# Constants behind the second load of x, and filter tables spread over the slots, in a Fourier filter with a soft mixture of experts

## The chip, the cores and the metric

The kernel runs on one core of one Trainium2 chip. The metric is the time of one execution in microseconds (us); three executions of the kernel before were timed. The profile is of one further execution. TensorE is PE in the profile, VectorE DVE, ScalarE ACT, GpSimd POOL, and SyncE, which issues nearly all transfers, SP.

## The reference

```python
def _attn_ref(x, filt_r, filt_i):            # x: (8, 2496, 256)
    X = np.fft.rfft(x, axis=1)
    Y = X * (filt_r + 1j * filt_i)[None, :, :]
    return np.fft.irfft(Y, n=x.shape[1], axis=1)

def _moe_ref(x, phi, w1, w2):                # x: the (19968, 256) rows of the above
    logits = x @ phi                         # 32 slots: 8 experts x 4
    d = softmax(logits, over all rows)       # written out in the original
    slot_input = d.T @ x
    slot_out = relu(slot_input[e] @ w1[e]) @ w2[e]   # for each expert e
    c = softmax(logits, over the slots)
    return c @ slot_out
```

Every sequence is filtered along its length in the frequency domain, and the result goes through a soft mixture of experts whose first softmax runs over all rows of all eight sequences.

## The kernel before, in words

The transform of length 2496 is done as 39 x 64. For each of the eight sequences ("batches" below, numbered from 0) there are three steps. First, eleven units `s1_unit(b, u)` (u = 0 to 10) multiply two blocks of x by a 39-point transform (line 305 for batch 0, in one matmul; line 308 for the others, in three matmuls of a high and a low part that `split_x` makes on ACT, line 294, and on POOL, line 295). Each unit's result is copied out of PSUM into a tile `at`, of which there are five, by ACT (line 312) or DVE (line 310), and written to a scratch array `a_dram` (line 316; the eleventh unit by lines 318 and 319). Second, ten "slots" per batch, `x_unit(b, c)`, each need one tile `ash` that `load_ash` reads back from `a_dram` (line 329) in another order. A read-back of a batch can start only when all of that batch's writes have landed, because every row of `ash` crosses all of them. The slot multiplies `ash` with `b_t` (line 339) and then with the filter tables `fr_t` and `fi_t` on DVE and POOL (lines 352 to 358). Third, `t_unit` (two slots later) transposes the result (line 366) and makes logits (line 377). Once a group of batches is through, a `chain` of small steps computes its softmax and its part of the slot inputs; it is advanced in hops, two per slot. At the end come the experts, and the blocks of the output are written out.

x comes in six loads per batch (`load_x`): each is a transfer of 112 rows and one of 5 rows, 448 and 20 KB (half of that for the sixth). Batch 0 has six buffers for them, the other batches share three (`XB`), so the fourth load waits until a buffer's two units have been split. `next_x` issues the next of these loads; it is called in the list below and after every second split.

Constants: `cst_t` (columns 0 to 128 hold the identity; 64.5 KB; the rest comes at slot 10, line 758), `b_t[:, 0]` (64 KB) and `be_t` (148 KB), from which `build_b` makes the other nineteen matrices of `b_t`, each by one ACT multiply (line 621) and one DVE operation (line 622). `build_minv` transposes the matrices of `b_t` on PE (line 628). `phi_t` and `fny_t` are small. The filter tables come in ten pairs (`load_tables`, lines 639 and 640; 128 KB for `fr_t`, 128 KB for `fi_t`); slot c uses pair c.

Two things set the order of the work. The string `STEPS` lists what is issued after each of the eleven units of batch 0, once before the units of batch 1, and after each of the five "slots" from -5 to -1, which run units 0 to 4 of batch 1. One word belongs to one place; a letter is I (identity), B (`b_t[:, 0]` and `be_t`), P (`phi_t`), F (`fny_t`), C (one `build_b`, two matrices), T (one pair of tables), X (`next_x`), A (one read-back of batch 0), and "-" for nothing. Tables that are left over (`late`) are loaded one pair per slot from slot 0. Besides, the kernel is built with a planner that orders each engine's instructions by their place in the program and by the time at which it thinks they can run; so an instruction can stand earlier on its engine than the program has it. Each engine, and SP's queue of transfers, then runs in the planned order and waits at the first instruction that isn't ready.

Of the kernel before, what the change touches and what calls it, by code (L numbers as in the profile page):

```python
# [9 lines left out]
F32 = mybir.dt.float32  # L10
# [3 lines left out]
AX = mybir.AxisListType  # L14
# [5 lines left out]
NT = 20  # L20
# [22 lines left out]
P = 128  # L43
SCALE = 2.0 / SEQ

XC = 4
# [13 lines left out]
WL = 5  # L60
SB = 3


STEPS = "IB P FC TC TC TC C XC C XC CC AA X - - - ATATAT"


def run_of(i, j):
# [152 lines left out]
def fft_soft_moe(ctx, tc, x, fr, fi, fny, phi, w1, w2, cst, w1q, bmat, out):  # L220
    nc = tc.nc
    pe, dve, act, pool_e, sp = nc.tensor, nc.vector, nc.scalar, nc.gpsimd, nc.sync
# [15 lines left out]
    cst_t = const.tile([P, CST.shape[1]], F32, name="cst_t")  # L238
    b_t = const.tile([P, NT, P], F32, name="b_t")
# [16 lines left out]
    def open_pool(name, bufs, side):  # L256
        cm = tc.tile_pool(name=name, bufs=bufs, side=side, reuse_waits="tile")
        return cm, cm.__enter__()
# [3 lines left out]
    x0_cm, x0p = open_pool("x0p", 6, "left")  # L262
# [9 lines left out]
    def load_x(b, c):  # L272
        pool = x0p if b == 0 else proda
        t = pool.tile([KR, XC, DIM], F32, tag="xt", name=f"xt{b}_{c}", bufs=6 if b == 0 else XB)
        i0 = c * XC
        n = min(XC, NI - i0)
        for lo, hi in ((0, RX), (RX, KR)):
            sp.dma_start(t[lo:hi, 0:n, :], x[b, lo:hi, i0 : i0 + n, :])
        xts[b, c] = t
# [5 lines left out]
    def split_x(b, u):  # L285

        c, k = divmod(2 * u, XC)
        xs = xts[b, c][:, k : k + 2, :]
        if b < FB:
            xhl[b, u] = xs, None  # L290
            return
        xh = proda.tile([KR, 2, DIM], F32R, tag="xh", name=f"xh{b}_{u}", bufs=3)
        xl = proda.tile([KR, 2, DIM], F32R, tag="xl", name=f"xl{b}_{u}", bufs=3)
        act.copy(xh, xs)  # L294
        pool_e.tensor_tensor(out=xl, in0=xs, in1=xh.bitcast(F32), op=ALU.subtract)  # L295
        xhl[b, u] = xh, xl
# [354 lines left out]
    def next_x():  # L651
        if xnext:
            load_x(*xnext.pop(0))

    def split_next(n):
        for b, u in at_slot.get(n, ()):
            split_x(b, u)
            if u % 2 == 1 or u == NH - 1:
                next_x()

    for c in range(6):
        load_x(0, c)
    if WM:
        warm = x0p.tile([P, 512], F32, name="warm", bufs=1)
        dve.memset(warm, 0.0)
        pw = ps_c.tile([P, 512], F32, tag="c", name="warm_up")
        for k in range(WM):
            pe.matmul(pw, warm[:, 0:P], warm, start=True, stop=True)
# [1 line left out]
    b_next = iter(range(CPB))  # L670
    ash_next = iter(range(ASH))
    issue = {
        "I": lambda: sp.dma_start(cst_t[:, 0 : P + 1], cst[:, 0 : P + 1]),
        "P": lambda: sp.dma_start(phi_t, phi.rearrange("(h q) e -> q h e", q=P)),
        "B": lambda: (sp.dma_start(b_t[:, 0], bmat[:, 0:P]), sp.dma_start(be_t, bmat[:, P:])),
        "F": lambda: sp.dma_start(fny_t, fny),
        "C": lambda: build_b(next(b_next)),
        "T": lambda: load_tables(next(tabs_next)),
# [2 lines left out]
    }  # L681
    steps = iter(STEPS.split())

# [2 lines left out]
            if token != "-":  # L686
                issue[token]()

    be_t = x0p.tile([P, 2 * P + 2 * NT], F32, name="be_t", bufs=1)
    split_x(0, 0)  # L690
    for u in range(NH):
        if u + 1 < NH:
# [58 lines left out]
    for n in range(NS + LT):  # L751
# [20 lines left out]
        if n >= LT:  # L772
            b, c = divmod(n - LT, CPB)
# [189 lines left out]
```

## Time and profile before

| | |
|---|---|
| timed executions | 431.23 us median (430.06 to 432.34, three) |
| profiled execution | 425.78 us, of which the span from the first to the last instruction is 423.9 us |
| busy share of the span | PE 88%, DVE 64%, ACT 52%, POOL 48% |
| mean granted TensorE clock | 0.944 of full speed |
| moved by transfers | 107.07 MB, 253 GB/s on average |

In rows of a timeline the first number is the start in us from the span's start, the second the length; "x12" stands for twelve instructions of one kind in a run. The rows of the chain of waits are pieces of the chain of work that ended last, followed back from the end of the kernel. In a table of stretches the share after the clock is the mean busy share of the 16 transfer engines; it can pass 1 a little.

### The profile page before, as it was taken

The page shows a single profiled execution, that of the slowest core. Times are in us where ns is not written, and L with a number is a line of the kernel's source. Part 1 is how long each engine was busy: PE and PEld are TensorE (multiplying, and loading weights), DVE is VectorE, ACT ScalarE, POOL GpSimd, SP SyncE. Part 2 cuts the span into 40 slices and gives each one's busy share as a digit, 9 for nine tenths or more (in the row PEclk, how much of TensorE's full clock was granted, in tenths as well). Part 3 has the DMA queues.
Part 4 walks back from the last instruction along what each step waited for, and adds up shares of the span by engine and source line. Part 5 has one row for each costly group of instructions (what it writes and reads, how often), then busy time and mean ns, then how long its engine had stood idle before and what let it go on. Part 6 is the DMA issues. An engine that isn't in the chain of part 4 may idle for free.

```text
span 423.9 us, 12672 instructions
## 1 busy us (share of the span) xinstructions
PE 374.5 (88%) x5065; PEld 291.3 (69%) x5065; DVE 269.8 (64%) x496; ACT 218.6 (52%) x475; POOL 201.9 (48%) x234
## 2 busy tenths in 40 slices
PE   7557998999999999999989999989998799999740
PEld 2225876788877787886867688778767435898730
DVE  1341764886989955878998387896378322787330
ACT  2465666676677656765792333461446121675320
POOL 0027778797768655965966056572200401750000
PEclk9688999999999999999999999999998999999555
DMA  8999999999889686978996524333199895699994
GB/s 209 238 306 288 331 321 327 334 294 344 246 262 337 213 264 206 289 214 256 269 280 167 186 82 121 101 103 101 55 344 347 268 275 185 249 394 381 386 362 166
DMA packets 61820, 107.07 MB, mean 253 GB/s; under 512 B 6142, under 2 KB 37758, under 8 KB 60226
## 3 DMA queue, kind: packets, MB, share of 16 engines
q1 hardware_dynamic: 61762, 106.26, 79.3%
q8 instruction: 40, 0.66, 0.6%
q14 instruction: 18, 0.15, 0.1%
HBM read 63.50 MB, written 42.74 MB: 251 GB/s over the span
## 4 chain that ended last, share of the span: by engine, by line
PE 61%; DMA 16%; DVE 12%; ACT 3%; issue 2%; SPq 2%; POOL 0%; ACTq 0%; DVEq 0%
PE x L339 15%; PE s L308 8%; PE t L366 6%; DMA out<-obr 6%; DMA xt<-in_x 6%; PE s L581 4%; PE l L377 4%; PE out L903 3%; PE v L423 3%; PE dt L537 2%; DMA ash<-a_dram 2%; DVE t L353 2%; PE o L833 2%; PE lg L450 2%; PE s L305 2%
## 5 line engine op out<-in xcount | busy, mean ns | idle before, releaser
L295 POOL TENSOR_TENSOR xl<-xt,xh 117x512 fp32r<-117x512 f32 x77 | 103.0, 1350 | 52.7 <-ACT xh L294 49.9
L339 PE MATMUL x<-b_t,ash 128*128 128x128 f32 x640 | 91.5, 284 | 6.1 <-DMA ash<-a_dram 3.1
L339 PEld LDWEIGHTS x<-b_t,ash 128*128 128x128 f32 x640 | 81.2, 194 | 17.0 <-issue 5.0
L356 POOL TENSOR_TENSOR yt<-yt,t 128x256 f32<-128x256 f32 x80 | 65.9, 826 | 40.7 <-DVE t L353 30.5
L352 DVE TENSOR_TENSOR yt<-x,fr_t 128x512 f32<-128x512 f32 x80 | 54.7, 684 | 39.9 <-PE x L339 36.9
L294 ACT CAST xh<-xt 117x512 fp32r<-117x512 f32 x77 | 46.8, 622 | 35.4 <-DMA xt<-in_x 12.1
L368 ACT COPY y<-t 128x512 f32<-128x512 f32 x80 | 46.5, 591 | 34.3 <-PE t L366 28.6
L312 ACT COPY at<-s 120x512 f32<-120x512 f32 x83 | 48.4, 587 | 21.7 <-PE s L305 8.6
L353 DVE TENSOR_TENSOR t<-x,fi_t 128x512 f32<-128x512 f32 x80 | 54.3, 678 | 0.0
L366 PE MATMUL t<-cst_t,yt 128*128 128x128 f32 x320 | 48.5, 276 | 0.7 <-POOL yt L356 0.4
L355 DVE TENSOR_TENSOR yt<-yt,t 128x256 f32<-128x256 f32 x60 | 43.3, 730 | 0.8
L366 PEld LDWEIGHTS t<-cst_t,yt 128*128 128x128 f32 x320 | 37.3, 141 | 7.9 <-issue 3.1
L308 PE MATMUL s<-xh,w1h 117*120 117x512 f32 x77 | 36.0, 468 | 6.5 <-ACT xh L294 5.5
L903 PE MATMUL out<-so_h,st 32*128 32x256 f32 (+1 forms) x320 | 36.3, 329 | 3.3 <-ACT obr L912 2.4
L903 PE MATMUL out<-so_l,st 32*128 32x256 f32 (+1 forms) x320 | 34.4, 311 | 0.0
L903 PEld LDWEIGHTS out<-so_h,st 32*128 32x128 f32 (+1 forms) x320 | 29.9, 206 | 6.5 <-ACT obr L912 3.0
L308 PE MATMUL s<-xl,w1h 117*120 117x512 f32 x77 | 32.2, 419 | 0.3 <-POOL xl L295 0.2
L308 PE MATMUL s<-xh,w1l 117*120 117x512 f32 x77 | 31.1, 404 | 0.0
L355 POOL TENSOR_TENSOR yt<-yt,t 128x256 f32<-128x256 f32 x20 | 16.2, 811 | 30.5 <-DVE t L353 24.2
L903 PEld LDWEIGHTS out<-so_l,st 32*128 32x128 f32 (+1 forms) x320 | 30.3, 209 | 0.0
L377 PE MATMUL l<-yt,phi_t 128*32 128x128 f32 x640 | 26.1, 278 | 0.9 <-ACT y L368 0.7
L912 DVE COPY ob<-out 128x512 f32<-128x512 f32 x32 | 20.6, 684 | 7.6 <-PE out L903 7.3
(118 smaller groups left out, 552.6 us busy)
## 6 DMA issues: line engine op xcount, KB each, us to landing
ash<-a_dram SPq DMA_DIRECT2D x80, 256.0 KB
a_dram<-at SPq DMA_DIRECT2D x80, 240.0 KB
xt<-in_x SPq DMA_DIRECT2D x40, 448.0 KB
w<-in_w SPq DMA_DIRECT2D x64, 256.0 KB
out<-ob SPq DMA_DIRECT2D x12, 1024.0 KB
out<-ob SPq DMA_DIRECT2D x8, 512.0 KB
out<-obr SPq DMA_DIRECT2D x8, 448.0 KB
xt<-in_x SPq DMA_DIRECT2D x8, 224.0 KB
```

The source lines that it names most:

```text
L294: act.copy(xh, xs)
L295: pool_e.tensor_tensor(out=xl, in0=xs, in1=xh.bitcast(F32), op=ALU.subtract)
L308: pe.matmul(ps, w, xx, start=(n == 0), stop=(n == 2))
L312: act.copy(at, ps)
L339: pe.matmul(ps[:, 2 * k + dh].rearrange("q r c -> q (r c)"), ash[:, k, dh * P : (dh + 1) * P], b_t[:, t0 + k, :], start=True, stop=True,)
L352: dve.tensor_tensor(out=yt, in0=ps, in1=frv, op=ALU.mult)
L353: dve.tensor_tensor(out=t2, in0=ps[:, :, ::-1, :], in1=fiv, op=ALU.mult)
L355: add.tensor_tensor(out=yt[:, :, 1, :], in0=yt[:, :, 1, :], in1=t2[:, :, 1, :], op=ALU.add)
L356: pool_e.tensor_tensor(out=yt[:, :, 0, :], in0=yt[:, :, 0, :], in1=t2[:, :, 0, :], op=ALU.subtract)
L366: pe.transpose(pt[:, k, dh, :], yt[:, c % 2, 2 * k + dh].rearrange("q r c -> q (r c)"), ident)
L368: act.copy(y, pt.rearrange("k p h d -> k p (h d)"))
L903: nc.tensor.matmul(prs[k][0:rows, mm, :], st[q, n // 2, c0 : c0 + rows], (so_h, so_l)[n % 2][q, :], start=(n == 0), stop=(n == 3),)
```

## The change

The identity, `b_t[:, 0]` and `be_t` are issued within the loop over the six loads of batch 0's x, behind the second load, instead of by the letters I and B after the first unit. The string is rewritten: one pair of tables stands ahead of the first two read-backs (by the string it was three), three more stand among the slots -4 to -1 (three before), and so six pairs instead of four are left for one per slot from slot 0 on. The letters X stand elsewhere, and there are four instead of three.

```diff
-STEPS = "IB P FC TC TC TC C XC C XC CC AA X - - - ATATAT"
+STEPS = "P F C C C C C XC C C CC XTAA AX T A X ATT"
...
+    be_t = x0p.tile([P, 2 * P + 2 * NT], F32, name="be_t", bufs=1)
     for c in range(6):
         load_x(0, c)
+        if c == 1:
+            sp.dma_start(cst_t[:, 0 : P + 1], cst[:, 0 : P + 1])
+            sp.dma_start(b_t[:, 0], bmat[:, 0:P])
+            sp.dma_start(be_t, bmat[:, P:])
...
     issue = {
-        "I": lambda: sp.dma_start(cst_t[:, 0 : P + 1], cst[:, 0 : P + 1]),
         "P": lambda: sp.dma_start(phi_t, phi.rearrange("(h q) e -> q h e", q=P)),
-        "B": lambda: (sp.dma_start(b_t[:, 0], bmat[:, 0:P]), sp.dma_start(be_t, bmat[:, P:])),
...
-    be_t = x0p.tile([P, 2 * P + 2 * NT], F32, name="be_t", bufs=1)
```

## The prediction

> **What bounds the kernel now.** I read the chain of waits first, for the stretch that the change touches (0 to 75 us):
>
> ```profile
> 1.23 0.33 SPq L278
> ...
> 2.32 0.33 SPq L278
> ...
> 2.69 6.71 DMA xt<-in_x
> ...
> 9.42 0.35 SPq L673
> ...
> 9.81 5.10 DMA b_t<-in_bmat
> ```
>
> ```profile
> 34.28 4.37 DMA ash<-a_dram
> ...
> 38.69 3.59 PE x L339 x16
> ...
> 54.53 5.98 DMA xt<-in_x
> ...
> 65.37 5.91 DMA ash<-a_dram
> ...
> 71.32 1.17 PE x L339 x8
> ```
>
> So the path runs through transfers up to 71 us. The first read-back is issued at 34.28, slot 0 begins at 38.69; the read-back for slot 10 (batch 1) is issued at 65.37 and its matmuls begin at 71.32. Then the order of SP's transfers:
>
> ```profile
> 0.74 0.44 SPq L232 DMA_DIRECT2D w1q_t<-in_w1q  x1
> 1.23 6.72 SPq L278 DMA_DIRECT2D xt<-in_x  x12
> 9.42 0.35 SPq L673 DMA_DIRECT2D cst_t<-in_cst  x1
> 9.81 0.43 SPq L675 DMA_DIRECT2D b_t<-in_bmat  x1
> 11.49 0.33 SPq L675 DMA_DIRECT2D be_t<-in_bmat  x1
> ...
> 13.69 0.37 SPq L316 DMA_DIRECT2D a_dram<-at  x1
> ...
> 28.40 0.39 SPq L319 DMA_DIRECT2D a_dram<-at  x1
> 28.84 0.30 SPq L278 DMA_DIRECT2D xt<-in_x  x1
> 29.61 0.36 SPq L639 DMA_DIRECT2D fr_t<-in_fr  x1
> ...
> 33.10 0.75 SPq L278 DMA_DIRECT2D xt<-in_x  x2
> 33.89 0.35 SPq L640 DMA_DIRECT2D fi_t<-in_fi  x1
> 34.28 0.90 SPq L329 DMA_DIRECT2D ash<-a_dram  x2
> ...
> 60.53 0.28 SPq L319 DMA_DIRECT2D a_dram<-at  x1
> ```
>
> The transfer issued at 2.69 is the sixth (`w1q_t`, then four of x at 1.23 to 2.32). It lands at 9.40, and only then, at 9.42, goes the fourteenth: SP holds an issue until the one eight places earlier has landed. `b_t` goes at 9.81 and takes 5.10 us, behind x. All six pairs of tables of `STEPS` stand ahead of the first read-back at 34.28: the planner pulled the three of "ATATAT" forward into SP's wait for the last write of 28.40.
>
> What that does to the engines:
>
> ```profile
> PE minv L628 <- DMA b_t<-in_bmat: 5.4, 1, 5.4
> ```
>
> PE's queue holds the first transpose for `build_minv` (line 628) between units 3 and 4, so PE stands 5.4 us for `b_t` although x is there. It looks like the price of the old order. Whether it is shows in the table of stretches:
>
> ```profile
> 3.00:12.00 9.00, 6.63 (x13) 2.16 (x11) 0.70 (x2) 1.17 (x2) 0.00 (x0) 0.98 1.03 265
> 12.00:18.00 6.00, 2.96 (x5) 1.35 (x6) 1.74 (x5) 2.05 (x6) 0.00 (x0) 0.50 0.88 215
> 18.00:30.00 12.00, 7.17 (x21) 3.35 (x20) 6.45 (x18) 7.64 (x22) 1.25 (x2) 0.93 0.98 302
> 30.00:36.00 6.00, 5.28 (x25) 3.88 (x24) 0.17 (x1) 5.82 (x12) 6.00 (x10) 0.82 0.86 265
> 36.00:60.00 24.00, 21.63 (x177) 18.41 (x176) 15.01 (x26) 12.73 (x25) 16.85 (x17) 0.93 1.02 318
> 60.00:75.00 15.00, 12.75 (x96) 8.80 (x94) 6.26 (x13) 10.71 (x22) 12.34 (x11) 1.00 1.03 334
> 75.00:100.00 25.00, 24.71 (x234) 20.61 (x235) 20.57 (x33) 17.89 (x37) 22.00 (x21) 1.00 1.04 324
> 100.00:160.00 60.00, 58.83 (x852) 48.44 (x854) 50.47 (x80) 39.84 (x83) 41.40 (x39) 1.00 0.87 270
> 160.00:340.00 180.00, 169.25 (x2758) 135.05 (x2756) 130.48 (x248) 89.25 (x200) 87.20 (x99) 0.99 0.65 199
> ```
>
> The first column is the stretch, then each engine's busy time, the clock, the share of the transfer engines, GB/s. From 3 to 100 us the transfers are full except in 12:18 (0.88) and 30:36 (0.86). PE is full from 75 us to 340 us (24.71 of 25, 58.83 of 60, 169.25 of 180), but in 60:75 it has 12.75 of 15. So up to slot 10 the transfers are the bound, and PE afterwards. The last write of batch 1 shows it too: it waits in SP's queue, for a load of x:
>
> ```profile
> SPq L319 <- DMA xt<-in_x: 1.2, 1, 1.2
> ```
>
> **The change part by part.** I count a gain only where it moves the 65.37 us at which slot 10's read-back is issued; PE carries the rest from there at its own pace, so what is won there is won at the end.
>
> Sizes, from the list of transfers:
>
> ```profile
> xt<-in_x SPq DMA_DIRECT2D x40, 448.0 KB
> ...
> fr_t<-in_fr SPq DMA_DIRECT2D x10, 128.0 KB
> ...
> be_t<-in_bmat SPq DMA_DIRECT2D x1, 148.0 KB
> ...
> cst_t<-in_cst SPq DMA_DIRECT2D x1, 64.5 KB
> b_t<-in_bmat SPq DMA_DIRECT2D x1, 64.0 KB
> ```
>
> *Constants moved.* Three issues leave the places 14 to 16 and take 6 to 8. Their issue takes 0.35 + 0.43 + 0.33 = 1.1 us of SP, in which SP would otherwise have waited for landings (9.42 waits on 9.40). They are moved past eight transfers of x. Their 276.5 KB (64.5, 64, 148) cost about 1.1 us at the 265 GB/s of 3:12, by which the third to sixth load of x come later; between 0.6 us (half) and 5.1 us (the whole landing of `b_t`, if small transfers hold up what follows). PE has that slack: it stood until `b_t` was there at 14.91. `b_t` should land near 9 us instead of 14.9, so PE's 5.4 us for it goes; next in line is x itself, two units per load, each load some 1.8 us at 265 GB/s, so PE goes on waiting, in smaller pieces. ACT and DVE can begin `build_b` some 6 us earlier, beside those waits. The first write of `a_dram` moves from 13.69 to about 11, when its turn of eight comes. On the transfers this wins only the hole of 12:18, which comes of three constants and two still smaller transfers (phi, fny) being in flight together: 0.12 x 6 = 0.7 us (bounds 0 and 0.7).
>
> *Fewer tables ahead of the first read-backs.* Up to 34.28 there were six pairs, 12 issues, 1.5 MB. The new string has four before slot 0, one ahead of the read-backs; the planner may again pull the others forward, so two to five pairs fewer, 0.52 to 1.31 MB, 1.7 to 4.3 us at the 302 GB/s of 18:30. With the 0.7 that brings the first read-back to between 29 and 32 us and slot 0 to 33.5 to 36.5 us. That is not yet won: the same bytes must be through before slot 10.
>
> *Tables one per slot.* Six pairs instead of four go in slots 0 to 5: four more issues of 0.36 us ahead of the writes of batch 1 and the loads of batch 2 in SP's queue, 0.52 MB, 1.6 us at 318 GB/s. What waits behind them are writes of `at`, and through them ACT's copies, and the read-back of slot 10. In sum to 65.37 the bytes are unchanged, so I put 0 for it; bounds -0.5 (the idle time of an issue filled) to +1.6. The tables themselves arrive in time: pair 4 + n is issued in slot n, four slots ahead, of (71.32 - 38.69) / 10 = 3.3 us each, against landings of 4.4 to 6 us in the rows above.
>
> *The hole of 30:36.* SP stands for the last write with the queue running dry: 0.14 x 6 = 0.84 us. Two effects: it can vanish as the writes end earlier and spread better, or grow, since tables were what filled SP's wait (28.84 to 33.89). Together with 0.02 x 12 = 0.24 us in 18:30 that is 1.1 us at stake; I take all of it, since the string still has an X and a T directly ahead of the read-backs and the writes of batch 1 to follow. Bounds: gain 1.1, loss 4.2 (below).
>
> *The fourth X.* There are three buffers; a load can't start before its buffer is free, so one more letter only puts it earlier in the order. 0, bounds 0.5 either way (one issue of about 0.3 us and its neighbour).
>
> Sum: 0.7 + 1.1 + 0 + 0 = 1.8 us won of the profiled 425.78 (span 423.9 and 1.9 around it), which would be 424.0. The runs shown have a median of 431.23, 5.4 us above the profiled execution; the same 1.8 taken from it gives **429.4 us**, -0.4%. What tells from no change in a measurement of this kernel is about 0.5%, 2.2 us, so the likeliest case lies close to that bound.
>
> **The rivals.**
>
> *PE's wait was the price* (chance 0.22). If read-backs and writes of batch 1 simply come earlier with PE, the whole 5.4 us arrive: 425.8 us. For it: the chain goes through `b_t`, and writes of `at` that lie in SP's queue go earlier. Against it: full transfers in 36:60 and 60:75.
>
> *Nothing moves* (0.18). The two holes close and others open, such as at slot 10, where the later tables stand ahead of batch 1's writes: 431.2 us. For it: the bytes don't change. Against: the hole of 12:18 has a plain cause that is removed.
>
> *SP stands at the first read-back without filling* (0.15, the slower case). Between the last write (28.40) and the read-back (34.28) the rows show issues of x and of tables: six tables of 128 KB and one load of x, 1.26 MB, 4.2 us at 302 GB/s. If the queue has nothing to send there, these 4.2 us are idle and the bytes come after slot 0, on a bound that is full. With the 0.7 won before: +3.5, 434.7 us; it decides when 2.9 of the 4.2 us are empty (2.2 + 0.7), from which on the case is over 0.5% slower.
>
> *Small transfers hold up the queue* (0.05). The constants take 5.1 us from issue to landing as a train, and the third load of x waits for all of it: then units 4 to 10 begin no earlier than the 14.91 of now, the 0.7 is not won, and 1.1 is left: 430.1. The Trainium skill, "DMA: Bandwidth & Descriptors" (Anatomy of one DMA, and Measured), speaks for that: for transfers that GpSimd issues it gives a fixed part of about 2.0 us each and advises batches of 1 MiB or more. As an estimate by that page, three transfers served singly would take 6.6 us. By that rule 6.6 us would fall on x. The trace agrees only in part: the share of 1.03 in 3:12, with transfers of 10 to 448 KB in flight, shows them overlapping.
>
> **How the numbers follow.** The forecast has 0.40, with 427.5 to 431.0 as its own range (gain of the two holes doubled, or nearly lost). Of it some 0.18 lie beyond 0.5% faster; with the first rival that is 0.40 and I say 0.41. Slower: 0.15 and a few per cent of the others, 0.18. The remaining 0.41 is no change. The range reaches to the first rival (425.8, less 0.3) and toward the slower one: 425.5 to 433.6, which leaves out about half of each of these two, 2 in 10.
>
> **What would show each step.** PE's wait of line 628 for `b_t` is under 1.5 us, and `b_t` lands near 9 us. The share of 12:18 is 0.95 or more. The first read-back is issued between 29 and 32 us. The read-back for slot 10 is issued at 63 to 64.5 us, and PE waits more than 2.3 us in the 15 us ahead of it (15 - 12.75 now). From there to the end the distance is as before. The prediction is wrong if slot 10's read-back moves with PE by 4 us or more (first rival), or if the share in the 6 us ahead of the first read-back falls under 0.5 (slower case), or if PE loses time after 100 us, which no step here touches.

## The result, and the profile after

The changed kernel is not faster, as forecast, but slightly slower: the ratio of its time to that of the kernel before is 1.0064 with an interval of 1.0037 to 1.009, medians 430.5 against 429.61 us over 20 executions of each. In a second series on another occasion it was 1.0017 (0.9977 to 1.0057); the two, weighted by their intervals, give 1.0050 (1.0028 to 1.0072), about 2.1 us. The ratios leave out executions over 1.5% above the fastest of the same kernel, six of the profiles below are of such ones, and two readings hang on it: by the means of all executions the change is at 1.0027 (0.9993 to 1.0061), not clear of noise, and the fourth load with a buffer (below) at 1.0080 and not at 1.0038. The profiled execution took 432.04 us, its span is 429.9 us.

In the rows of the changed kernel all line numbers of the loop bodies are one lower (L338 is the old L339). Its chain of waits, for the first 110 us:

```profile
3.56 4.86 DMA be_t<-in_bmat
...
15.47 4.28 DMA xt<-in_x
...
19.83 0.04 ACT xh L293
...
20.36 0.59 ACT at L311
...
32.14 5.09 DMA ash<-a_dram
...
37.28 1.43 PE x L338 x8
...
62.42 5.55 DMA xt<-in_x
...
71.34 1.35 PE x L338 x8
...
101.04 7.09 DMA xt<-in_x
```

SP's order of transfers at the places that the prediction speaks of:

```profile
2.69 0.35 SPq L664 DMA_DIRECT2D cst_t<-in_cst  x1
3.08 0.43 SPq L665 DMA_DIRECT2D b_t<-in_bmat  x1
...
12.26 0.36 SPq L315 DMA_DIRECT2D a_dram<-at  x1
...
27.26 0.35 SPq L318 DMA_DIRECT2D a_dram<-at  x1
...
32.14 1.52 SPq L328 DMA_DIRECT2D ash<-a_dram  x3
...
65.12 3.14 SPq L328 DMA_DIRECT2D ash<-a_dram  x4
```

What PE waited for in the first 39 us:

```profile
PE s L304 <- ACT at L311: 3.8, 3, 3.1
PE x L338 <- DMA ash<-a_dram: 1.7, 1, 1.7
...
PE minv L627 <- DVE b_t L621: 0.2, 1, 0.2
```

So the first part went nearly as said: `be_t` has landed by 8.42 us, the 5.4 us for `b_t` are gone, the first read-back goes at 32.14 instead of 34.28, and slot 0 begins 1.4 us earlier. In place of `b_t`, PE now waits 3.8 us for ACT's copies. The longest of these waits ends at 20.99: in the chain above, the load of x issued at 15.47 lands, a split on ACT (L293) takes it at 19.83, and only behind that comes the copy of 20.36 that PE waits for. Then hardly anything comes of it at slot 10: its read-back goes at 65.12 (65.37 before) and PE begins it at 71.34 (71.32). From there on this profile loses. The table of stretches, with the same columns as in the prediction:

```profile
3.00:12.00 9.00, 8.40 (x18) 3.42 (x17) 3.19 (x11) 3.56 (x12) 0.00 (x0) 1.00 1.05 272
12.00:18.00 6.00, 5.55 (x12) 1.59 (x10) 4.20 (x13) 3.71 (x11) 0.00 (x0) 1.00 1.01 290
18.00:30.00 12.00, 8.53 (x26) 4.26 (x27) 1.38 (x2) 7.30 (x15) 6.22 (x7) 0.86 1.01 325
30.00:36.00 6.00, 4.59 (x18) 2.41 (x16) 0.00 (x0) 4.43 (x9) 4.55 (x7) 1.00 0.98 306
36.00:60.00 24.00, 21.50 (x177) 18.45 (x178) 15.10 (x25) 14.19 (x28) 17.72 (x17) 0.93 1.02 316
60.00:75.00 15.00, 12.80 (x89) 8.86 (x86) 7.52 (x12) 8.00 (x16) 9.41 (x9) 0.89 0.99 294
75.00:100.00 25.00, 24.18 (x216) 20.21 (x217) 20.63 (x34) 16.29 (x34) 20.10 (x19) 1.00 1.04 321
100.00:160.00 60.00, 56.30 (x826) 46.38 (x824) 47.99 (x78) 38.19 (x81) 40.59 (x37) 1.00 0.87 259
160.00:340.00 180.00, 168.54 (x2761) 134.49 (x2763) 130.24 (x249) 91.05 (x205) 88.44 (x100) 1.00 0.65 197
```

Both holes of the transfers are closed (12:18 from 0.88 to 1.01, 30:36 from 0.86 to 0.98), and PE loses where the prediction had it full: 0.5 us in 75:100 (24.18 against 24.71) and 2.5 us in 100:160 (56.30 against 58.83). PE waits there for ACT and for DVE. First ACT. A piece of ACT's timeline of the changed kernel, in brackets the idle time before and what ended it:

```profile
101.74 0.30 ACT L383 COPY lt<-l 128x128 f32<-128x128 f32 x1
104.34 1.14 ACT L293 CAST xh<-xt 117x512 fp32r<-117x512 f32 x2 [2.30 <-DMA xt<-in_x]
105.39 0.58 ACT L311 COPY at<-s 120x512 f32<-120x512 f32 x1
105.87 0.59 ACT L367 COPY y<-t 128x512 f32<-128x512 f32 x1
108.82 0.62 ACT L293 CAST xh<-xt 117x512 fp32r<-117x512 f32 x1 [2.36 <-DMA a_dram<-at]
109.34 0.54 ACT L429 COPY v<-v 128x462 f32<-128x462 f32 x1
```

and of PE's in the same stretch:

```profile
106.51 0.65 PE L376 MATMUL l<-yt,phi_t 128*32 128x128 f32 x16 [0.65 <-ACT y L367]
...
109.93 0.90 PE L422 MATMUL v<-minv_t,lsb 128*32 128x66 f32 x48 [0.92 <-ACT v L429]
```

ACT's queue holds a split of x (L293) ahead of copies that PE needs now. The split waits 2.3 us for its x, and the copies of `y` and `v` wait behind it, and PE behind these. ACT's waits for x in 75 to 165 us add up (total, number, longest) to 5.2 us before:

```profile
ACT xh L294 <- DMA xt<-in_x: 5.2, 6, 1.7
```

and to 10.9 us after, with 2.4 us more that the profile puts down to another transfer and that I take to be of the same kind:

```profile
ACT xh L293 <- DMA xt<-in_x: 10.9, 8, 2.3
ACT xh L293 <- DMA a_dram<-at: 2.4, 1, 2.4
```

Of PE's waits over 0.2 us in 75 to 165 us, the two for ACT make 1.6 us (0.7 and 0.9). The longest single one is for DVE:

```profile
PE t L365 <- DVE yt L354: 2.1, 1, 2.1
```

It ends at 144.39 us, and the chain of waits shows what stood ahead on DVE: two subtractions of the `chain` (L487, L603), between and behind which come the filter steps of the slots:

```profile
135.10 3.16 DVE d L487 x3
...
139.46 2.15 DVE lg L603 x2
...
142.80 1.45 DVE yt L354
...
144.39 0.63 PE t L365 x4
```

The second profile of the changed kernel has the same wait of 2.1 us; in the two of the kernel before PE's waits for DVE there are 0.2 us.

Why the split stands there is seen in the order that the planner made of each program. Counting PE's instructions, 53 units of batches 1 to 7 stand ahead of slot 40 (the first of batch 4) in the kernel before, 56 in the changed one. That order is fixed in the program: ACT's and DVE's too is the same in both profiles of the kernel before, and another in both of the changed one, far behind the place of the edit. By the description of the planner above, the edit changed it because the planner places each instruction by when it expects its inputs; what it expected is not on record.

The two profiles differ by 6.0 us of span, more than the times do. Of this 3.0 us are there at the first matmul of the experts (342.97 against 339.97), and the rest arises in the output, which moves from one execution to the next (below). Neither repeats: the second pair of profiles has 341.44 against 343.30 at the experts and spans of 424.2 against 430.4 us. PE's loss in 100:160 does repeat (56.69 against 58.01), that in 75:100 does not (24.95 against 24.35). And a part of it is no loss, since PE has done more by then:

```profile
0.00:39.00 39.00, 24.08 (x65) 11.89 (x66) 10.21 (x28) 19.62 (x45) 9.38 (x16) 0.87 0.91 256
```

in the kernel before, and in the changed one

```profile
0.00:39.00 39.00, 30.22 (x82) 14.13 (x83) 10.12 (x29) 21.90 (x49) 12.43 (x19) 0.94 0.96 285
```

### The profile page after: what moved, and what is told of

Read it like the earlier page. It is cut to its first block, busy times and chain, and to the rows that moved or that the text cites. A ratio compares the mean times of both kernels' runs of the same rounds, so it can differ in the third digit from the quotient of the medians.

```text
span 429.9 us, 12668 instructions
## 1 busy us (share of the span) xinstructions
PE 379.8 (88%) x5065; PEld 292.9 (68%) x5065; DVE 269.2 (63%) x496; ACT 218.2 (51%) x475; POOL 201.7 (47%) x234
## 4 chain that ended last, share of the span: by engine, by line
PE 57%; DVE 16%; DMA 16%; ACT 3%; issue 3%; SPq 1%; POOL 0%; ACTq 0%; DVEq 0%
PE x L338 14%; PE s L307 8%; DMA out<-obr 6%; PE t L365 6%; DMA xt<-in_x 5%; PE s L580 4%; PE out L904 4%; PE l L376 3%; DMA ash<-a_dram 3%; DVE t L352 3%; PE v L422 2%; DVE yt L351 2%; DVE yt L354 2%; PE lg L449 2%; DVE d L487 2%
## 5 line engine op out<-in xcount | busy, mean ns | idle before, releaser
L338 PE MATMUL x<-b_t,ash 128*128 128x128 f32 x640 | 91.1, 284 | 6.6 <-DMA ash<-a_dram 1.7
L338 PEld LDWEIGHTS x<-b_t,ash 128*128 128x128 f32 x640 | 81.1, 194 | 16.8 <-issue 4.9
L293 ACT CAST xh<-xt 117x512 fp32r<-117x512 f32 x77 | 46.8, 624 | 36.7 <-DMA xt<-in_x 18.0
L904 PE MATMUL out<-so_h,st 32*128 32x256 f32 (+1 forms) x320 | 38.4, 338 | 6.4 <-ACT obr L913 5.3
L904 PEld LDWEIGHTS out<-so_h,st 32*128 32x128 f32 (+1 forms) x320 | 31.5, 215 | 9.0 <-ACT obr L913 6.0
L904 PE MATMUL out<-so_l,st 32*128 32x256 f32 (+1 forms) x320 | 36.3, 319 | 0.0
L904 PEld LDWEIGHTS out<-so_l,st 32*128 32x128 f32 (+1 forms) x320 | 31.9, 217 | 0.0
```

The lines of the kernel that those rows point to most:

```text
L338: pe.matmul(ps[:, 2 * k + dh].rearrange("q r c -> q (r c)"), ash[:, k, dh * P : (dh + 1) * P], b_t[:, t0 + k, :], start=True, stop=True,)
L904: nc.tensor.matmul(prs[k][0:rows, mm, :], st[q, n // 2, c0 : c0 + rows], (so_h, so_l)[n % 2][q, :], start=(n == 0), stop=(n == 3),)
```

## The experiments

The theories: the *fourth load* (one X more puts loads and units of later batches ahead in the planned order); the *constants* (`build_minv`'s transposes, now ahead of unit 2 in PE's queue, upset what follows); the *tables* (late ones are in the way); *chance* (two single executions differ). All ratios are against the kernel before.

**The changed kernel again, and the kernel before again**

> The changed kernel once more, to see which of its losses repeat. In the two profiles at hand it begins slot 0 1.4 us earlier than the kernel before (37.3 against 38.7), slot 10 at the same time, slot 79 3.3 us later (293.5 against 290.2), and ends 6.0 us later, so 2.7 us more in the output. Fourth-load theory and constants theory: the 3.3 us up to slot 79 repeat to 1 us, since they come of the order of the instructions. Chance theory (the difference lies in states of single executions): slot 79 moves by more than 2 us. All theories: the 2.7 us of the output may be of one execution only. Time against before: ratio 1.004 to 1.009 by the first two, 0.997 to 1.009 by the last.

> The kernel before once more, for how far a single profile moves: slots 10, 40 and 79 within 1.5 us of 71.3, 168.4 and 290.2 us; the output from its first matmul (359.9) to the end (423.9) may differ by 6 us, as it did between the two profiles of the changed kernel.

Measured: the changed kernel 1.0017 (0.9977 to 1.0057), with a span of 424.2 us, slot 10 at 70.0 and slot 79 at 292.0. The ratio lies below what I had put down for an effect of the order (1.004 to 1.009) and in the range for chance (0.997 to 1.009). The kernel before (one further profile) has a span of 430.4, slots 10, 40 and 79 at 72.1, 170.8 and 293.8. So slot 79 of one and the same kernel moves by 3.6 us from execution to execution, more than I had allowed (1.5), and slot 79 of a single profile can't decide between the theories, though I had set bounds by it. From the first output matmul to the end it took 64.1 and 65.2 us in the two profiles of before, 66.8 and 63.0 in those of the changed kernel: the 2.7 us in the output were of one execution. What repeats is ACT's wait for x, 5.2 and 5.7 us in the two profiles before, 10.9 and 9.1 us after, and PE's wait of 2.1 us for DVE. In what follows the ratios decide, and ACT's waits and PE's busy time say where.

**Constants alone** (edit against the changed kernel)

```diff
-STEPS = "P F C C C C C XC C C CC XTAA AX T A X ATT"
+STEPS = "- P FC TC TC TC C XC C XC CC AA X - - - ATATAT"
```

> Constants behind the second load of x, the string of the kernel before (without I and B). Constants theory (the transposes of build_minv now stand ahead of unit 2 and upset what follows): the whole loss, ratio 1.005 to 1.01, slot 79 at 292 to 294 us, PE busy 56 to 57.5 of the 60 us in 100 to 160. Fourth-load theory: no loss, ratio 0.995 to 1.002, slot 79 at 288 to 290.5, PE busy 58.5 or more of 60 there. Both: slot 10 within 1 us of 71.3, and PE's wait of 5.4 us for b_t is gone.

> The constants alone once more, to narrow the interval of 0.9936 to 1.0. The prediction's sum (1.8 us of 430, 0.9958) holds if the ratio lies in 0.993 to 0.999; no gain if it lies at 0.999 or above. Slot 10 at 69 to 70 us (71.3 and 72.1 before), for a read-back that goes some 2 us earlier.

Measured: 0.9968 (0.9936 to 1.0), and in the repetition 0.9952 (0.9904 to 1.0); weighted together 0.9963 (0.9936 to 0.9990), a gain of 1.6 us. The constants theory falls. Units ahead of slot 40: 53, as before. Slot 10 is at 69.2 and 70.9 (71.3 and 72.1 before), the first further from 71.3 than the 1 us that I had allowed. Its read-back is at 63.8 and 64.8 (65.4 and 66.2), 1.5 us earlier on average, which agrees with the time; but two profiles of each can't show it by themselves, since in the three of the next kernel that read-back goes at 65.4, 66.2 and 61.5.

```profile
12.00:18.00 6.00, 5.70 (x13) 1.87 (x12) 4.07 (x13) 4.16 (x12) 0.00 (x0) 1.00 0.90 241
...
30.00:36.00 6.00, 4.47 (x19) 2.46 (x17) 0.00 (x0) 5.87 (x13) 5.33 (x7) 0.99 1.03 323
```

In this profile of the constants alone the hole of 12:18 is hardly smaller (0.90), the hole of 30:36 is gone (1.03). The second profile agrees (0.85 and 1.02). But the second profile of the kernel before has 0.95 in 30:36, so a part of that hole was of one execution. PE was busy for 58.4 of the 60 us in 100 to 160, between the two expectations; slot 79, at 292.0, lay where the constants theory had it, but slot times don't decide here.

**The changed kernel without its fourth X** (edit against the changed kernel)

```diff
-STEPS = "P F C C C C C XC C C CC XTAA AX T A X ATT"
+STEPS = "P F C C C C C XC C C CC XTAA AX T A - ATT"
```

> The changed kernel without the fourth X (the one after slot -2 is taken out), so that loads of x are issued as early as in the kernel before. Fourth-load theory (one load earlier lets the planner put the units of line 307 some three units earlier in PE's queue, and PE stands there for x in 75 to 160 us): the loss goes, ratio 0.994 to 1.002, slot 79 at 288.5 to 291, no wait of PE or ACT for x over 5 us near 101 us, PE busy 58 or more of the 60 us in 100 to 160. Constants theory: loss stays, ratio 1.004 to 1.01, slot 79 at 292.5 to 294.5. Tables theory (late tables are in the way): loss stays too.

> The changed kernel without the fourth X once more, for a second profile, since the first was of a disturbed execution. Fourth-load theory: slot 79 at 289 to 292 us, and ACT's waits for x in 75 to 165 us under 7 us. Else slot 79 again at 294 or later.

> The changed kernel without its fourth X once more, for the interval: constants and tables as in the change, 54 units ahead of slot 40. If tables placed so cost nothing of their own and the constants gain: 0.993 to 0.999, the same as the constants alone to 0.3%. If the tables take the gain back: 0.999 to 1.003.

Measured: 0.9971 (0.9933 to 1.0009) and 0.9947 (0.9891 to 1.0003), together 0.9963 (0.9932 to 0.9995). The loss is gone, and the gain is that of the constants alone. 54 units stand ahead of slot 40. Slot 79 came at 294.8, 290.6 and 291.4. The wait of ACT for x in 75 to 165 us, of the second and the third profile:

```profile
ACT xh L293 <- DMA xt<-in_x: 3.1, 3, 1.4
```

```profile
ACT xh L293 <- DMA xt<-in_x: 3.9, 4, 1.8
```

One letter, issued at slot -2, is worth 0.9% of the whole time (1.0050 against 0.9963). Tables placed as in the change cost nothing when this letter is out.

**The kernel before with a fourth X**

```diff
-STEPS = "IB P FC TC TC TC C XC C XC CC AA X - - - ATATAT"
+STEPS = "IB P FC TC TC TC C XC C XC CC AA X - - X ATATAT"
```

> The kernel before with a fourth X (after slot -2), nothing else. Fourth-load theory: the loss appears without the constants and tables, ratio 1.004 to 1.01, slot 79 at 292 to 294.5 us, a wait for x of more than 5 us in 95 to 130 us. Constants theory and tables theory: ratio 0.998 to 1.003, slot 79 at 289 to 291.

Measured: 1.0146 (1.0091 to 1.0202), 6.2 us, above the range of 1.004 to 1.01 that I had put down, and three times the loss of the changed kernel. 58 units stand ahead of slot 40.

```profile
ACT xh L294 <- DMA xt<-in_x: 13.0, 8, 3.2
```

**The new string alone, constants at their old place**

```diff
-STEPS = "IB P FC TC TC TC C XC C XC CC AA X - - - ATATAT"
+STEPS = "IBP F C C C C C XC C C CC XTAA AX T A X ATT"
```

> The new string of the changed kernel with the constants left at their old place (I and B in front of its first P). Fourth-load theory, with the constants themselves a gain of 0.3%: the loss is here and larger than in the changed kernel, ratio 1.007 to 1.016, ACT's waits for x (line 294) over 9 us in 75 to 165 us, against 5.2 in the kernel before. If the tables that come later are a gain of their own: less than the 1.0146 of the kernel before with a fourth X, by 0.3% or more; if they are a loss: more by as much. If the loss of the changed kernel needed the constants at the new place: ratio 0.997 to 1.003.

Measured: 1.0101 (1.0056 to 1.0145); 59 units ahead; ACT's waits for x 11.0 us. The loss doesn't need the constants at the new place. Whether the tables gain or lose beside the fourth X is not told by 1.0101 against 1.0146, since the intervals overlap.

**Tables alone**

```diff
-STEPS = "IB P FC TC TC TC C XC C XC CC AA X - - - ATATAT"
+STEPS = "IB P FC C C C C XC C XC CC TAA X - - - ATATAT"
```

> The kernel before with only the tables moved: one pair ahead of the first read-backs and three at slot -1, six late (TAA X - - - ATATAT), three X as before, constants at their old place. In the planned order 58 units of line 307/308 stand ahead of slot 40 in PE's queue here, as with the fourth X (58), against 53 in the kernel before. The prediction's term for tables (nothing, the bytes are the same) and the theory that it is the letter X as such: ratio 0.997 to 1.004, ACT's waits for x in 75 to 165 us 4 to 7 us. The theory that any edit costs which puts splits and units ahead of their loads in the planned order: ratio 1.007 to 1.016, ACT's waits for x over 9 us.

Measured: 1.0117 (1.0052 to 1.0182), 5.0 us, with three X and the constants where they were. So it is not the letter X as such. By the string three pairs of tables no longer stand ahead of the first X, and the planner again puts more units ahead, as it would if it thought that x comes earlier: 58 units, and

```profile
ACT xh L294 <- DMA xt<-in_x: 12.2, 8, 3.7
```

**The fourth load with a buffer of its own**

```diff
-XB = 3
+XB = 4
...
-YB = 34
+YB = 32
```

once on the kernel before with a fourth X, once on the changed kernel. `YB` counts the buffers of `y`, which later hold weights of the experts; two of them make room for the fourth buffer of x.

> The kernel before with a fourth X and with four buffers for it (XB = 4; to make room, ypool has 32 buffers and not 34, which concerns weights after 290 us). The theory that the loss comes of ACT's splits standing earlier in its order than x can land, since the earlier load has no buffer to go to: with a buffer of its own the load goes out at once, ACT's waits for x in 75 to 165 us fall back under 7 us and the ratio to 0.993 to 1.004. The theory that transfers are simply full in that stretch, whatever the buffers: the loss stays, ratio 1.009 to 1.018, ACT's waits stay over 10 us. The theory that it is PE's order alone (units of later batches ahead of slots): loss stays or grows, with ACT's waits small.

> The changed kernel with four buffers for its four X (XB = 4, ypool 32 buffers). Theory of ACT's splits waiting for a load without a buffer: the loss goes while the constants' gain stays, ratio 0.992 to 1.001, ACT's waits for x in 75 to 165 us under 6 us (9.1 and 10.9 in the changed kernel). Else ratio 1.002 to 1.01. In the planned order units stand even further ahead here (61 ahead of slot 40), so a theory of PE's order alone expects 1.005 or more.

Measured: 1.0038 (1.0006 to 1.007) for the first, so that most of 1.0146 goes; 1.006 (1.0009 to 1.0111) for the second, no better than the changed kernel and outside of what I had put down for this theory (0.992 to 1.001). ACT's waits for x in 75 to 165 us go in both, in the first to

```profile
ACT xh L294 <- DMA xt<-in_x: 3.3, 5, 1.3
```

and in the second to

```profile
ACT xh L293 <- DMA xt<-in_x: 0.8, 2, 0.5
```

So in the second the time does not follow ACT's waits for x in this stretch. Where it goes instead is not shown. 61 units stand ahead of slot 40, and in 39 to 75 us PE is busy for 28.08 us of 36,

```profile
39.00:75.00 36.00, 28.08 (x241) 22.12 (x241) 19.78 (x35) 20.19 (x41) 25.68 (x24) 1.00 0.98 310
```

where the kernel before had

```profile
39.00:75.00 36.00, 33.75 (x269) 26.91 (x267) 21.27 (x38) 21.78 (x44) 27.27 (x26) 0.95 1.02 326
```

with ACT waiting there for writes of `at` and for x:

```profile
ACT at L311 <- DMA a_dram<-at: 6.3, 3, 2.5
ACT xh L293 <- DMA xt<-in_x: 6.1, 5, 2.4
```

Neither wait belongs to this kernel alone: in the same stretch the changed kernel with three buffers waits 6.5 us for writes of `at`, and the constants alone, which gain, 6.4 us for x. The two buffers of `y` are a rival that I did not separate. From the first matmul of the experts to the first of the output both kernels with four buffers take 22.1 us, the other twelve profiles 19.8 to 21.9 us, 20.5 on average; that is 1.6 us of losses of 1.6 and 2.6 us. A run with `YB = 32` alone is missing.

PE's busy time in 100 to 160 us separates the kernels with three buffers. The seven profiles of those with 53 and 54 units ahead have 58.0 us or more, the five of the others 57.6 or less. The time of the first matmul of the experts shows the loss of the three slowest, 347.9 to 349.5 us, and with a fourth buffer the first of them is back at 342.8; the change lies within the 340.0 to 343.3 us of the kernel before.

| kernel | units ahead of slot 40 | ACT's waits for x, 75 to 165 us | PE busy, 100 to 160 us | first matmul of the experts, us | ratio |
|---|---|---|---|---|---|
| before | 53 | 5.2, 5.7 | 58.8, 58.0 | 340.0, 343.3 | 1 |
| constants alone | 53 | 5.0, 7.0 | 58.4, 58.6 | 341.6, 341.5 | 0.9968, 0.9952 |
| change without the fourth X (waits: second and third profile) | 54 | 3.1, 3.9 | 59.0, 59.0, 59.0 | 343.0, 338.8, 341.0 | 0.9971, 0.9947 |
| the change | 56 | 10.9, 9.1 | 56.3, 56.7 | 343.0, 341.4 | 1.0064, 1.0017 |
| before with a fourth X | 58 | 13.0 | 57.6 | 348.2 | 1.0146 |
| tables alone | 58 | 12.2 | 56.6 | 349.5 | 1.0117 |
| string alone | 59 | 11.0 | 56.7 | 347.9 | 1.0101 |
| before, fourth X, fourth buffer | 62 | 3.3 | 59.3 | 342.8 | 1.0038 |
| change, fourth buffer | 61 | 0.8 | 58.9 | 343.0 | 1.006 |

With three buffers the loss appears with the units ahead: none at 53 and 54, 0.5% at 56, 1.0 to 1.5% at 58 and 59. Units done ahead are work that need not be done later, which is why slot times alone overstate a loss: in the first pair of profiles slot 40 of the change came 5.2 us late and slot 60 only 3.0 us, in the second pair slot 40 came 1.4 us late and slot 60 1.8 us early. With four buffers 61 and 62 units stand ahead and the loss is 0.4 to 0.6%, so the count alone does not set it.

## Why the prediction was wrong

*The moved constants: right in sum, in part by luck.* For the whole change 1.8 us were forecast; the constants alone measured 1.6 (0.4 to 2.8). `b_t` landed early, and PE's 5.4 us went without showing up as 5.4 us. I put 0.7 of the 1.8 on the hole of 12:18, as the constants' own. With the constants alone that hole stayed (0.90 and 0.85), so the small transfers in flight together were not its whole cause; it closed in both profiles of the change, with the new string. The 1.1 on the holes behind it have a basis, since 30:36 closed (1.03 and 1.02), but with 0.86 and 0.95 before it is worth some 0.6 us on average, and the rest of the 1.6 us is not placed.

*The fourth X: the step that failed.* I gave it "0, bounds 0.5 either way", because a load can't start before its buffer is free. That looks at the load alone; the letter also moves what is planned behind it. Added to the kernel before it measured 6.2 us, within the change about 0.9%, 3.7 us. Without it the change gains 1.6 us, near the 1.8 of the forecast.

*The tables: right for this change, for a reason that does not hold.* "In sum to 65.37 the bytes are unchanged, so I put 0 for it", with a bound of 1.6. With the constants at the new place and three X they cost nothing: 0.9963 with the tables moved, and 0.9963 with the constants alone. Alone they measured 5.0 us, with the same bytes and the same signs as the fourth X: 58 units ahead and ACT's waits of 12.2 us. That the 0 held here is luck.

*"From there to the end the distance is as before".* Here the error has its place. I had shown that PE is full from 75 us on and took what it waits for there as fixed. It is not: the order of its queue, of ACT's and of DVE's was planned anew, and PE lost 2.5 and 1.3 us in 100 to 160 in the two pairs of profiles. This is the last of the signs by which the prediction named itself wrong: PE loses time after 100 us, "which no step here touches".

*The level.* The 430.5 us measured lie in the forecast's own range of 427.5 to 431.0, but only because the forecast started from 431.23 us of three executions; twenty gave 429.61.

*First read-back and slot 0.* 32.14 and 37.3 us against 29 to 32 and 33.5 to 36.5: a little late. Between the write of 27.26 and the read-back SP again issued tables and loads, so the slower rival (SP stands without filling) didn't come about: 30:36 has a share of 0.98.

*The rivals.* "PE's wait was the price" fell: slot 10 did not move with PE. "Nothing moves" comes near to slot 10 (its read-back at 65.12 and 65.19 against 65.37 and 66.23), but not for its reason: the holes closed, and no share under 0.97 opened up to 75 us in the two profiles. That small transfers hold up the queue does not fit the share of 1.05 in 3:12, nor unit 4, the first to need the third load, which was issued right behind the constants: it began at 13.96 us, ahead of the 14.91 that the rival set. What came about instead, work planned ahead of its data, was none of my rivals, although the prediction said that the planner had pulled tables forward.

*What stays open.* That the fourth X turns the gain into a loss is shown by taking it out. That more units ahead go with a loss was seen in four kernels with three buffers. That ACT's waits for x carry it is argued from the rows above: a buffer more takes these waits away in two kernels, and with them, by the ratios, the larger part of the loss in one of the two. In the change itself PE waits longer for DVE (2.1 us) than for ACT (1.6 us). How the loss divides between ACT, DVE, the five `at`, SP's queue and, with four buffers, the two buffers of `y` was not separated. A kernel that keeps the new string and holds the old order of the splits wasn't tried.

## What to carry to other kernels

Where a planner orders the queues, an edit in the first 20 us is an edit of the whole program: compare the planned order of PE, ACT and SP far behind the edit before pricing it, and count how much later work stands ahead of each consumer. A queue that runs in order makes an early instruction dangerous when its data is late, since the copies behind it wait too; here a load that was issued earlier, on full transfers, came with longer waits for it (ACT's rose from 5.2 to 13.0 us with the fourth X). And a bundle of edits should be taken apart: here the constants gain 0.4%, and a letter in a string, which looks like nothing, takes back twice as much; the change without its fourth X (0.9963, 0.9932 to 0.9995) is faster than both kernels.

## What the runs showed that was not expected

The output phase, the same instructions on the same data, took 62.1 to 67.5 us from its first matmul to the end of the span in the fourteen profiles, with the shortest in one of the constants alone; the same kernel twice, the change, gave 66.8 and 63.0. Slot 79 of the kernel before came at 290.2 and 293.8 us in two executions. A reading of one profile against one other is worth little under 4 us here, and early stages are no exception: slot 10 came within 0.8 us in the two profiles of the kernel before, but at 72.6, 71.0 and 68.3 in the three of the change without its fourth X.
